# Attention and gated MLP on one core: the first keys loaded in two parts, identity transposes while the first data are on their way

## The chip, the core and the metric

The kernel runs on one core of a Trainium2 chip. TensorE (PE) multiplies and transposes, VectorE (DVE), ScalarE (ACT) and GpSimd (POOL) do the elementwise work, SyncE (SP) issues nearly all DMA transfers. The metric is the device time of one execution in microseconds; less is better.

## What is computed

Two steps, all in float32: attention with queries that are averaged in pairs, and an MLP with a gate on its result.

```python
q_pool = q.reshape(4, 8, 576, 2, 64).mean(axis=3)          # q, k, v: 4 batches, 8 heads, 1152 x 64
scores = 1 / np.sqrt(64) * (q_pool @ k.transpose(0, 1, 3, 2))
attn = np.exp(scores - scores.max(-1, keepdims=True))
attn = attn / (attn.sum(-1, keepdims=True) + 1e-9)
x = (attn @ v)                                             # put together to 2304 tokens x 512
h = x @ w_in                                               # 512 x 2048
out = (h * np.clip(h + 3, 0, 6) / 6) @ w_out               # 2048 x 512
```

## The kernel before

Two heads make a pair; there are 16 pairs g, four in each batch. Of a pair, `load_k`, `load_q` and `load_v` fetch keys `kr` (128 partitions x 9 rows x 2 heads x 64), queries `qr` and values `vr`. `pool_q` adds neighbouring queries to `qp`, `turn_q` transposes them on PE (six transposes into PSUM), `keep_q` copies the result to `qh`; `turn_k` and `keep_k` do the same with the keys (nine transposes, `kT`). `scores` multiplies one of nine key tiles with 288 queries of both heads into a PSUM tile `pv`; `keep` copies it to `s` on ACT, and `most` keeps the running maximum `m` on DVE. When nine tiles are through, `fold`, `best` and `spread` (PE, DVE, PE: `pst`, `mq`) take the maximum over the keys, `lessen` subtracts it (DVE or POOL), `expo` is the exponential on ACT, and `values` multiplies with `vr` into `pav`.

The first five pairs (EARLY = 5) run in this form, three PSUM tiles `pv` wide. In the same stretch the two weight matrices are converted: for 16 blocks f and two halves, `load_raw` fetches `raw`, and `convert` has seven steps: ACT makes the absolute value, POOL clamps it, DVE does three passes over bits in a PSUM tile, then ACT or POOL rounds and POOL subtracts; `save_w` writes `w_d`. For f below 12 these three DVE passes use a `pv` tile.

After the maxima of the fifth pair and the conversions of the first twelve blocks a step `second_step` gives the PSUM of `pv` to other tiles. From there the other eleven pairs run in another form (`pqk`, `pt`), and between their steps the layers of the MLP (`do_layer`, tile `ph`; `do_project`, tile `po`). After the last pair only MLP layers are left.

The order of all this is set by a planner. `arrange` lists every step with a place (from tables of numbers: START, SLOPE, AT, ATL, BIAS and so on), its cost on each engine that may do it, the steps it needs, and the buffers it takes and frees. `Order.run` plays this list through in time: an engine that is free takes, of the steps that are ready and have room, the one with the lowest place. The instructions are then written down in that order, and each engine works its own list in order; a waiting instruction holds up all behind it.

In the first pair nine keys come in one load of two transfers (one for each head, on SP's queue), the queries in one transfer that ACT issues. `turn_k` of the first five pairs is split in six and three tiles, since one PSUM tile holds six. In the listing `load_raw` for f = 0 needs the step `lq` of pair 0 to be placed.

Of the kernel before, what the change touches and what calls it, by code (L numbers as in the profile page):

```python
# [11 lines left out]
F32 = mybir.dt.float32  # L12
# [9 lines left out]
SWEEPS = ((0, 0, 8), (1, 0, 8), (0, 8, 16), (1, 8, 16), (2, 0, 16), (3, 0, 16), (4, 0, 16), (5, 0, 16))  # L22
START = (477.66, 415.01, 302.76, 744.89, 190.23, 357.45, 457.74, 517.76)
SLOPE = (-25.05, 17.09, -28.37, -75.02, 10.14, 11.96, 19.53, -7.47)
LAG = 21.74
MLP = (-241.92, 155.01, -282.2, -587.9)
CONV = 836.78
CSTEP = (77.41, -722.1)
NEAR = 5
EARLY, FCV = 5, 12  # L30
BIAS = (-271.81, -258.65, 75.37, -576.39, 171.43, 165.5)
CUT = 8
PER = (13.78, 18.27)
AT = (104.48, -27.88, 1.45, 269.18, -487.99, 83.52, -374.87, 520.32, -503.94, -3.26, -120.1, 156.6, -61.98, 354.49)
ATL = (36.18, -16.61, -201.47, 878.58, 286.63, 413.95, -133.32, -449.41, 489.14, 426.77, 869.98, 263.26, 385.08, 499.61)
TAIL = 768
QUEUED = True
STICK = 0.2926
# [9 lines left out]
class Order:  # L48
# [10 lines left out]
    def run(self):  # L59
# [11 lines left out]
        back, out, t, wires = [], [], 0.0, 0.0  # L71
# [10 lines left out]
        while len(out) < len(steps):  # L82
# [4 lines left out]
            for e in engines:  # L87
# [17 lines left out]
                if e == "PE":  # L105
                    more, kind = SHIFT.get((kind, cost[e][3]), 0), cost[e][3]
                    busy, end = busy + more, end + more
                    while work and work[0][1] < t - SPELL:
                        work.pop(0)
                    idle = SPELL - sum(max(0.0, min(y, t) - max(x, t - SPELL)) for x, y in work)  # L110
                    if not slow:
                        slow = t > 16000 and idle > IDLE
                        since = t
                    elif t - since >= SPELL and idle < 340:
                        slow = False
                    if slow:
                        busy, end = 2 * busy, end + busy
                    work.append((t, t + busy))
# [37 lines left out]
def arrange(od, do, B=4, NPAIR=4, KT=9, KC=3, NH=2, NFC=16, NT=2304, P=128, HQ=288, SQ=576):  # L156
# [8 lines left out]
    for g in range(NG):  # L165
# [3 lines left out]
        early = g == 0  # L169
        add(("lk", g), lead + at[11], {"SP": (940, 6500, 2600)}, do("load_k", g=g), (), ("kr",))  # L170
        add(("lq", g), lead + at[12], {"SP": (470, 6900, 2000)}, do("load_q", g=g), (), ("qr",))
        z = lead + at[0]
# [5 lines left out]
        for c in C3 if late else range(2):  # L178
            n = 3 if late or c else 6
            add(("tk", g, c), z + 2 + c, {"PE": (100 * n, 100 * n + 250, 0, "t") if late else (160 * n, 160 * n + 300, 0, "t")}, do("turn_k", g=g, c=c),  # L180
                [("tk", g, c - 1)] if c else [("lk", g)] + [("second",)] * (g == NEAR), ("v" if g < NEAR else "s",),
                ("kr",) if c == (2 if late else 1) else ())
# [17 lines left out]
        for h in range(NH):  # L200
            for j in range(2):
# [3 lines left out]
                if late or j == 0:  # L205
                    before = (g, h, 0) if j else (g, h - 1, late) if h else (g - 1, NH - 1, g - 1 >= EARLY) if g else None
                    for t in range(KT):
# [3 lines left out]
                            ([("mm", u, t - 1)] if t else [("mm", before, KT - 1)] if before else [])  # L211
                            + ([("ql", g, h, j) if late else ("qh", g, 0, 0)] if not t else []) + [("kl", g, t // KC) if late else ("kh", g, t // 6)]
                            + ([("second",)] if late and not t else []),
# [138 lines left out]
def pooled_attention_then_gated_mlp(ctx, tc, q, k, v, w_in, w_out, out):  # L352
# [5 lines left out]
    KC = 3  # L358
# [122 lines left out]
    with ExitStack() as a:  # L481
# [32 lines left out]

        def load_k(eng, g):
            kr_t[g] = ld.tile([P, KT, 2, D], F32, tag="kr", name="kr", bufs=1)
# [36 lines left out]
        def space(g, *shape):  # L553
# [3 lines left out]
            return ps_m["s"].tile([P] + list(shape), F32, tag="s", name="pt")  # L557

        def turn_k(eng, g, c):
            if g < EARLY:  # L560
                ps = room_v()[:, :, 0:KC * P].rearrange("p b (t k) -> p b t k", k=P)
                to = [ps[:, t // KC, t % KC, :] for t in range(6)]
                ts = range(6 * c, min(6 * c + 6, KT))
            else:
# [7 lines left out]
        def keep_k(eng, g, c):  # L572
# [5 lines left out]
            if g < EARLY:  # L578
                n = 1 if c else 2
                to = kT[g][:, 6 * c:6 * c + KC * n].rearrange("p (b t) k -> p b (t k)", t=KC)  # L580
                copy(eng, to, ps[:, 0:n].rearrange("p b t k -> p b (t k)"))
                return
# [425 lines left out]
```

## Time and profile before

| | |
|---|---|
| time, median of 3 runs | 872.42 us (872.12 to 872.78) |
| the profiled execution: time, span | 872.05 us, 870.0 us |
| mean granted clock of PE | 0.987 |
| PE busy in the span | 837.8 us (96%) |
| DVE busy | 666.7 us (77%) |
| ACT busy | 574.4 us (66%) |
| POOL busy | 507.5 us (58%) |

A busy time is the time in which at least one instruction of the engine is under way. Matmuls are pipelined and their ends are modelled, so a busy PE can still be one that could do more. The span runs from the first to the last instruction; the 2.05 us between it and the time of the execution lie around it. Shares are means over stages that have different limits, so the profile has to be read stretch by stretch.

### The profile page before, as it was taken

Reading aid. Unit: us, or ns where it says so; the run is one execution under the profiler, and the core shown is the slowest. Engines: PE = TensorE matmul, PEld = TensorE weight load, DVE = VectorE, ACT = ScalarE, POOL = GpSimd, SP = SyncE. Lnnn points to the kernel's source line nnn. Section 1 sums busy time; section 2 is a strip of 40 time slices with the busy share of each in tenths; the row PEclk is TensorE's granted clock in tenths of the full one; section 3 lists DMA queues with packets and bytes.
Section 4 is the critical chain, followed back from the end, with each engine's and each line's share of the span. In section 5 each row is a group of like instructions: output and inputs, shape, how many; then the busy total and the mean of one; then the engine's idle time right before and its main releaser. Section 6 shows DMA issues by size and latency. Waiting matters only on the chain.

```text
span 870.0 us, 16219 instructions
## 1 busy us (share of the span) xinstructions
PE 837.8 (96%) x5668; PEld 648.7 (75%) x5668; DVE 666.7 (77%) x1318; ACT 574.4 (66%) x1222; POOL 507.5 (58%) x457
## 2 busy tenths in 40 slices
PE   4899999999999999999999999999999999999997
PEld 3445555556888886888888878888888877888886
DVE  3898999987999989888889898888988973222222
ACT  3789897885777776767767777777767754222222
POOL 1756777775876785678568867787655766000000
PEclk9699999989999999999999999999999999999999
DMA  9878675569976896799777968898766748343423
GB/s 232 290 238 252 220 221 185 197 222 290 311 243 223 252 324 191 242 282 332 220 247 252 287 206 251 283 293 273 218 204 223 240 147 295 121 131 118 139 99 95
DMA packets 108976, 197.66 MB, mean 227 GB/s; under 512 B 46176, under 2 KB 63584, under 8 KB 108896
## 3 DMA queue, kind: packets, MB, share of 16 engines
q1 hardware_dynamic: 108208, 195.26, 70.3%
q10 hardware_dynamic: 688, 1.38, 0.5%
q8 instruction: 45, 0.74, 0.3%
q14 instruction: 35, 0.29, 0.1%
HBM read 168.82 MB, written 27.79 MB: 226 GB/s over the span
## 4 chain that ended last, share of the span: by engine, by line
PE 68%; DVE 11%; POOL 7%; issue 7%; ACT 5%; DMA 2%; SPq 0%; DVEq 0%; POOLq 0%; ACTq 0%
PE ph L408 20%; PE po L441 14%; PE pav L726 12%; PE pqk L630 10%; PE pt L441 5%; DVE m L648 4%; POOL d L719 3%; PE pv L626 3%; DVE s L701 2%; ACT s L535 2%; ACT s L709 1%; POOL gl L426 1%; PE pt L604 1%; PE pt L570 1%; DMA raw<-in_moe_w_out_dram 1%
## 5 line engine op out<-in xcount | busy, mean ns | idle before, releaser
L709 ACT ACTIVATE s<-s 128x864 f32<-128x864 f32 x192 | 177.2, 931 | 19.7 <-DVE s L701 17.8
L408 PE MATMUL ph<-mxmxh,w 128*128 128x256 f32 x896 | 180.8, 285 | 1.0 <-DVE r L417 0.7
L701 DVE TENSOR_TENSOR s<-s,pst 128x864 f32<-128x864 f32 x168 | 173.8, 1043 | 1.8 <-ACT mb L535 1.2
L535 ACT COPY s<-pqk 128x288 f32<-128x288 f32 x396 | 143.6, 403 | 39.5 <-PE pqk L630 37.5
L648 DVE TENSOR_TENSOR m<-pqk,m 128x288 f32<-128x288 f32 x308 | 138.1, 448 | 28.3 <-ACT s L535 17.9
L726 PE MATMUL pav<-s,vr 128*64 128x288 f32 x1152 | 155.3, 415 | 0.7 <-DVE x L797 0.6
L408 PEld LDWEIGHTS ph<-mxmxh,w 128*128 128x128 f32 x896 | 146.5, 190 | 4.4 <-DVE r L417 2.0
L413 ACT ACTIVATE r<-ph,three 128x256 f32<-128x256 f32 (+1 forms) x128 | 64.1, 501 | 114.4 <-PE ph L408 112.3
L441 PE MATMUL po<-w,gh 128*128 128x512 f32 x448 | 139.2, 392 | 0.0
L408 PE MATMUL ph<-mxmxl,w 128*128 128x256 f32 x448 | 126.4, 282 | 0.0
L726 PEld LDWEIGHTS pav<-s,vr 128*64 128x64 f32 x1152 | 77.8, 138 | 59.2 <-issue 12.1
L417 DVE SCALAR_TENSOR_TENSOR r<-r,ph 128x256 f32<-128x256 f32 (+1 forms) x128 | 56.8, 444 | 84.9 <-ACT r L413 84.4
L719 POOL TENSOR_TENSOR d<-s 128x864 f32<-128x864 f32 x44 | 91.0, 2069 | 52.5 <-ACT s L709 52.5
L630 PE MATMUL pqk<-qh,kT 128*128 128x288 f32 x396 | 119.6, 318 | 2.1 <-DVE m L648 1.9
L426 POOL TENSOR_TENSOR gl<-r,gh 128x256 fp32r<-128x256 f32 x96 | 70.9, 739 | 68.8 <-ACT gh L421 68.5
L630 PE MATMUL pqk<-ql,kT 128*128 128x288 f32 x396 | 110.8, 294 | 0.0
L441 PEld LDWEIGHTS po<-w,gh 128*128 128x128 f32 x448 | 84.3, 188 | 14.4
L441 PE MATMUL po<-w,gl 128*128 128x512 f32 x224 | 90.6, 404 | 1.5 <-DMA w<-w_d 1.0
L630 PEld LDWEIGHTS pqk<-qh,kT 128*128 128x128 f32 x396 | 74.6, 188 | 23.1 <-issue 7.9
L719 POOL TENSOR_TENSOR d<-d,s 128x864 f32<-128x864 f32 x44 | 90.1, 2048 | 1.6 <-ACT s L709 0.6
L408 PEld LDWEIGHTS ph<-mxmxl,w 128*128 128x128 f32 x448 | 85.2, 190 | 1.0
L421 ACT CAST gh<-r 128x256 fp32r<-128x256 f32 (+1 forms) x128 | 55.7, 435 | 32.7 <-DVE r L417 27.0
(107 smaller groups left out, 1415.9 us busy)
## 6 DMA issues: line engine op xcount, KB each, us to landing
w<-w_d SPq DMA_DIRECT2D x224, 512.0 KB, 5.0
w_d<-scratch SPq DMA_DIRECT2D x32, 512.0 KB, 4.6
kr<-in_k_dram SPq DMA_DIRECT2D x32, 288.0 KB, 6.2
vr<-in_v_dram SPq DMA_DIRECT2D x16, 576.0 KB, 4.3
qr<-in_q_dram SPq DMA_DIRECT2D x15, 576.0 KB, 7.3
raw<-in_moe_w_in_dram SPq DMA_DIRECT2D x16, 512.0 KB, 4.1
raw<-in_moe_w_out_dram SPq DMA_DIRECT2D x16, 512.0 KB, 5.9
mxmxh<-xh_d SPq DMA_DIRECT2D x5, 512.0 KB, 6.6
```

The source lines that it names most:

```text
L408: nc.tensor.matmul(ps, w[:, wi, cs], x[:, c, :], start=(m == 0), stop=(m == 3 * NCC - 1))
L413: nc.scalar.activation(out=r6, in_=ps, func=AF.Relu, bias=three)
L417: nc.vector.scalar_tensor_tensor(out=out, in0=r6, scalar=6.0, in1=ps, op0=ALU.min, op1=ALU.mult)
L426: on.tensor_tensor(out=gl, in0=r6, in1=gh.bitcast(F32), op=ALU.subtract)
L441: nc.tensor.matmul(o, g[:, ts], w[:, wi, :], start=(first and n == 0), stop=(last and n == 2))
L535: nc.scalar.copy(out=out, in_=in_)
L630: nc.tensor.matmul(ps[:, 0:HQ], kT[g][:, j, t, :], w[:, j, :], start=(m == 0), stop=(m == 1))
L648: nc.vector.tensor_tensor(out=m, in0=ps, in1=s0 if t == 1 else m, op=ALU.max)
L701: by[eng].tensor_tensor(out=s, in0=s, in1=m.unsqueeze(1).to_broadcast([P, KC, HQ]), op=ALU.subtract)
L709: nc.scalar.activation(out=s, in_=s, func=AF.Exp, scale=SCALE)
L719: by[eng].tensor_tensor(out=out, in0=x, in1=y, op=ALU.add)
L726: nc.tensor.matmul(av_t[g, h][j * D:(j + 1) * D, :], vr_t[g][:, j, t, :], s_t[g, h][:, j, t, :], start=(t == 0), stop=(t == KT - 1),)
```

## The change

The first pair gets its own loads. `load_k` takes a range of key tiles; for pair 0 there are two loads, tiles 0 to 2 (step `l0`) and tiles 3 to 8 (`lk`), each of two transfers. `first_k` splits the transposes and copies of pair 0 in three and six tiles instead of six and three. The place of `turn_q` in pair 0 is put ahead. A new step `warm` writes 36 transposes of the identity into a `pv` tile that nothing reads. The raw load of block 0 no longer needs `lq` of pair 0. All tables of the planner have new numbers, and with them the order of the whole program; the stretch at the start in which the planner does not count with a slow PE is 8 us instead of 16.

```diff
-START = (477.66, 415.01, 302.76, 744.89, 190.23, 357.45, 457.74, 517.76)
+START = (319.41, 415.74, 585.3, 658.57, 427.45, 490.94, 433.17, 512.16)
...
-SPELL, IDLE = 3413, 1600
+SPELL, IDLE, COLD = 3413, 1600, 8000
...
-                        slow = t > 16000 and idle > IDLE
+                        slow = t > COLD and idle > IDLE
...
+        if early:
+            add(("wu",), -1000, {"PE": (6400, 6400, 0, "t")}, do("warm"), (), ("v",), ("v",))
+            add(("lq", g), -1000, {"SP": (100, 5700, 1900)}, do("load_q", g=g), (), ("qr",))
+            add(("l0",), -999, {"SP": (800, 4500, 700)}, do("load_k", g=g, t0=0, t1=KC), (), ("kr",))
+            add(("lk", g), -998, {"SP": (800, 7000, 1300)}, do("load_k", g=g, t0=KC, t1=KT))
+        else:
+            add(("lk", g), lead + at[11], {"SP": (940, 6500, 2600)}, do("load_k", g=g), (), ("kr",))
+            add(("lq", g), lead + at[12], {"SP": (470, 6900, 2000)}, do("load_q", g=g), (), ("qr",))
...
-            n = 3 if late or c else 6
+            n = 3 if late or c != early else 6
...
-            z = place(g) + 2 * UNIT * h - at[1]
+            z = -900 if early else place(g) + 2 * UNIT * h - at[1]
...
-            add(("lr", f, h), z - 8, {"SP": (470, 6300, 1700)}, do("load_raw", f=f, half=h), ([("mm", (0, 0, 0), 2)] if f else [("lq", 0)]) + ([("cv", f - 2, 1 - h, 4)] if f > 1 else []), (f"raw{h}",))
+            add(("lr", f, h), z - 8, {"SP": (470, 6300, 1700)}, do("load_raw", f=f, half=h), ([("mm", (0, 0, 0), 2)] if f else []) + ([("cv", f - 2, 1 - h, 4)] if f > 1 else []), (f"raw{h}",))
...
-                nc.sync.dma_start(out=kr_t[g][:, :, j, :], in_=k[b, h].rearrange("(p t) d -> p t d", p=P))
+                nc.sync.dma_start(out=kr_t[g][:, t0:t1, j, :], in_=k[b, h].rearrange("(p t) d -> p t d", p=P)[:, t0:t1])
+
+        def warm(eng):
+            v = room_v()
+            for x in range(36):
+                nc.tensor.transpose(v[:, 0, 0:P], ident, ident)
...
+        def first_k(g, c):
+            cuts = (0, KC if g == 0 else 2 * KC, KT)
+            return cuts[c], cuts[c + 1]
```

What this does to the instructions is shown at three places. A row is one or more instructions of one engine in the order in which it works them, with line, operation, output and inputs, shape and count. The lines of the changed kernel are up to 16 higher.

PE at the start of the program, before: transposes of the keys and queries of pair 0, then its scores, and the first `fold`.

```order
L570 MATMUL pv<-ident,kr 128x128 x9
L599 MATMUL pv<-ident,qp 128x96 x6
L626 MATMUL pv<-qh,kT 128x288 x24
L674 MATMUL pst<-ident,m 96x128 x3
L626 MATMUL pv<-qh,kT 128x288 x4
```

And now:

```order
L531 MATMUL pv<-ident 128x128 x36
L586 MATMUL pv<-ident,kr 128x128 x3
L615 MATMUL pv<-ident,qp 128x96 x6
L586 MATMUL pv<-ident,kr 128x128 x6
L642 MATMUL pv<-qh,kT 128x288 x22
```

The 36 transposes stand first, the queries' transposes stand between the two parts of the keys.

ACT at the start, before (L535 is the copy helper, L856 the first step of a conversion):

```order
L535 COPY kT<-pv 128x768
L535 COPY kT<-pv 128x384
L535 COPY s<-pv 128x2x288 x4
L856 ACTIVATE scratch<-raw 128x512
L535 COPY s<-pv 128x2x288
L856 ACTIVATE scratch<-raw 128x512
```

And now:

```order
L547 COPY kT<-pv 128x384
L547 COPY qh<-pv 128x576
L872 ACTIVATE scratch<-raw 128x512 x2
L547 COPY s<-pv 128x2x288 x3
L547 CAST scratch<-scratch 128x512
```

The copy of the queries came over from DVE, the larger copy of keys went to DVE, and the first step of both halves of block 0 now stands ahead of the first copy of scores instead of behind the fourth.

DVE from the start of its work on pair 0, before (L648 is the maximum, L864, L869 and L873 the three passes of a conversion):

```order
L545 TENSOR_TENSOR qp<-qr 96x6x64 x2
L537 COPY qh<-pv 128x576
L648 TENSOR_TENSOR m<-pv,s 128x576
L648 TENSOR_TENSOR m<-pv,m 128x576 x3
L864 TENSOR_SCALAR pv<-scratch 128x512
L648 TENSOR_TENSOR m<-pv,m 128x576
```

And now:

```order
L557 TENSOR_TENSOR qp<-qr 96x6x64 x2
L549 COPY kT<-pv 128x768
L880 TENSOR_SCALAR pv<-scratch 128x512
L885 SCALAR_TENSOR_TENSOR pv<-raw,pv 128x512
L664 TENSOR_TENSOR m<-pv,s 128x576
L889 SCALAR_TENSOR_TENSOR scratch<-raw,pv 128x512
```

Two passes of a conversion moved ahead of the first maximum.

## Rows read from the trace of the kernel before

**Rows 1.** Windows: us, busy PE, PEld, DVE, ACT, POOL, PE clock, DMA share, GB/s.
```profile
0.00:19.19 19.19, 9.61 (x43) 6.99 (x43) 5.93 (x20) 7.00 (x11) 1.53 (x8) 1.00 1.03 260
19.19:175.00 155.81, 146.09 (x1140) 79.53 (x1140) 144.19 (x225) 132.51 (x230) 110.14 (x104) 0.96 0.70 224
...
190.00:720.00 530.00, 523.68 (x3653) 431.38 (x3652) 461.31 (x974) 381.96 (x884) 374.40 (x326) 1.00 0.79 252
```

**Rows 2.** Timelines, first 18 us: start, us, engine, line, out<-in, count [idle before].
```profile
1.01 0.29 POOL masks.py:199 TENSOR_SCALAR_AFFINE_SELECT ident<-ident 128x128 f32<-128x128 f32 x1
...
5.57 1.02 DVE L545 TENSOR_TENSOR qp<-qr 96x384 f32<-96x384 f32 x2 [2.91 <-DMA qr<-in_q_dram]
...
8.26 2.15 PE L570 MATMUL pv<-ident,kr 128*128 128x128 f32 x9 [8.26 <-DMA kr<-in_k_dram]
...
12.32 6.49 PE L626 MATMUL pv<-qh,kT 64*128 64x288 f32 x28 [0.94 <-DVE qh L537]
...
13.69 0.64 ACT L535 COPY s<-pv 128x576 f32<-128x576 f32 x1 [2.69 <-PE pv L626]
...
15.32 0.76 DVE L648 TENSOR_TENSOR m<-pv,s 128x576 f32<-128x576 f32 x1 [3.15 <-ACT s L535]
...
17.10 0.67 ACT L856 ACTIVATE scratch<-raw 128x512 f32<-128x512 f32 x1
...
17.86 0.61 POOL L858 TENSOR_SCALAR scratch<-scratch 128x512 f32<-128x512 f32 x1 [16.55 <-ACT scratch L856]
```

**Rows 3.** Windows over the first loads; the last number is GB/s.
```profile
0.00:8.00 8.00, 0.00 (x0) 0.00 (x0) 2.15 (x15) 1.28 (x1) 0.70 (x6) 1.00 0.89 179
8.00:10.00 2.00, 1.74 (x9) 1.77 (x10) 0.00 (x0) 0.19 (x1) 0.00 (x0) 1.00 1.09 373
```

**Rows 4.** PE: scores at 16 to 18 and 18 to 20, transposes, a window.
```profile
L626 PE MATMUL pv<-qh,kT 64*128 64x288 f32 x12 | 2.9, 636 | 0.0
...
L626 PE MATMUL pv<-qh,kT 64*128 64x288 f32 x6 | 1.1, 444 | 0.0
...
37.12 1.17 PE L599 MATMUL pv<-ident,qp 96*128 96x96 f32 x6
...
38.42 1.15 PE L570 MATMUL pv<-ident,kr 128*128 128x128 f32 x9
...
38.00:39.00 1.00, 1.00 (x11) 1.00 (x10) 0.59 (x1) 0.95 (x3) 0.63 (x1) 0.87 0.99 351
```

**Rows 5.** DVE groups by shape, 0 to 175 us; the page's exponential group.
```profile
L701 DVE TENSOR_TENSOR s<-s,pst 128x864 f32<-128x864 f32 x33 | 34.1, 1044 | 0.9 <-ACT mb L535 0.9
L864 DVE TENSOR_SCALAR pv<-scratch 128x512 uint32<-128x512 uint32 x24 | 16.5, 688 | 3.6 <-POOL scratch L858 2.3 <-ACT s L535 0.3
...
L537 DVE COPY qh<-pv 128x576 f32<-128x576 f32 x3 | 2.2, 740 | 4.8 <-PE pv L599 4.8
L537 DVE COPY x<-pav 128x288 f32<-128x288 f32 x3 | 1.4, 450 | 0.0
...
L537 DVE COPY kT<-pv 128x768 f32<-128x768 f32 x1 | 0.9, 912 | 0.0
L537 DVE COPY kT<-pv 128x384 f32<-128x384 f32 x1 | 0.5, 544 | 0.0
...
L709 ACT ACTIVATE s<-s 128x864 f32<-128x864 f32 x192 | 177.2, 931 | 19.7 <-DVE s L701 17.8
```

**Rows 6.** Around the change of stage: a window, and PE's timeline.
```profile
174.00:179.40 5.40, 3.73 (x35) 2.25 (x27) 5.02 (x11) 3.56 (x7) 3.30 (x4) 0.89 0.35 120
...
179.37 3.15 PE L726 MATMUL pav<-s,vr 128*64 128x288 f32 x12 [0.56 <-DVE x L797]
...
186.36 0.46 PE L696 MATMUL pst<-ident,mq 96*128 96x96 f32 x3
186.75 1.68 PE L726 MATMUL pav<-s,vr 128*64 128x288 f32 x12
```

**Rows 7.** DVE's waits from 19.19 to 175 us: total, times, longest.
```profile
DVE m L648 <- ACT s L535: 3.5, 7, 0.9
```

More of the change, by code (lines that the diff above doesn't have):

```diff
@@ L22 @@
 SWEEPS = ((0, 0, 8), (1, 0, 8), (0, 8, 16), (1, 8, 16), (2, 0, 16), (3, 0, 16), (4, 0, 16), (5, 0, 16))
-START = (477.66, 415.01, 302.76, 744.89, 190.23, 357.45, 457.74, 517.76)
[L24 to L28, printed above, removed]
+START = (319.41, 415.74, 585.3, 658.57, 427.45, 490.94, 433.17, 512.16)
+SLOPE = (-17.97, 17.36, -40.58, -56.66, 7.94, 4.7, 11.88, 16.54)
+LAG = 79.73
+MLP = (-210.77, 190.37, -107.71, -694.25)
+CONV = 933.83
+CSTEP = (104.43, -691.1)
 NEAR = 5
 EARLY, FCV = 5, 12
-BIAS = (-271.81, -258.65, 75.37, -576.39, 171.43, 165.5)
+BIAS = (-223.73, -414.45, -161.58, -399.1, 220.5, 285.78)
 CUT = 8
-PER = (13.78, 18.27)
-AT = (104.48, -27.88, 1.45, 269.18, -487.99, 83.52, -374.87, 520.32, -503.94, -3.26, -120.1, 156.6, -61.98, 354.49)
-ATL = (36.18, -16.61, -201.47, 878.58, 286.63, 413.95, -133.32, -449.41, 489.14, 426.77, 869.98, 263.26, 385.08, 499.61)
+PER = (14.57, 17.84)
+AT = (145.72, -51.21, 16.16, 71.58, -630.56, 61.99, -267.56, 606.83, -489.22, -59.04, -21.19, 134.2, -70.67, 375.86)
+ATL = (29.4, -7.25, -165.71, 932.44, 251.82, 417.4, -51.12, -468.16, 419.33, 340.1, 817.81, 256.61, 487.11, 656.69)
 TAIL = 768
 QUEUED = True
-STICK = 0.2926
+STICK = 0.2485
 CT = 256
@@ L178, in arrange @@
         for c in C3 if late else range(2):
-            n = 3 if late or c else 6
+            n = 3 if late or c != early else 6
             add(("tk", g, c), z + 2 + c, {"PE": (100 * n, 100 * n + 250, 0, "t") if late else (160 * n, 160 * n + 300, 0, "t")}, do("turn_k", g=g, c=c),
-                [("tk", g, c - 1)] if c else [("lk", g)] + [("second",)] * (g == NEAR), ("v" if g < NEAR else "s",),
+                ([("tk", g, c - 1)] if c else []) + [("l0",) if early and not c else ("lk", g)] * (early or not c) + [("second",)] * (g == NEAR and not c), ("v" if g < NEAR else "s",),
                 ("kr",) if c == (2 if late else 1) else ())
@@ L211, in arrange @@
                             ([("mm", u, t - 1)] if t else [("mm", before, KT - 1)] if before else [])
-                            + ([("ql", g, h, j) if late else ("qh", g, 0, 0)] if not t else []) + [("kl", g, t // KC) if late else ("kh", g, t // 6)]
+                            + ([("ql", g, h, j) if late else ("qh", g, 0, 0)] if not t else []) + [("kl", g, t // KC) if late else ("kh", g, t // (KC if early and t < 6 else 6))]
                             + ([("second",)] if late and not t else []),
@@ L513, in pair, with load_k @@
             return b, 2 * p + j
[L515 to L516 removed]
+        def load_k(eng, g, t0=0, t1=KT):
+            if t0 == 0:
+                kr_t[g] = ld.tile([P, KT, 2, D], F32, tag="kr", name="kr", bufs=1)
             for j in range(2):
                 b, h = pair(g, j)
[L519 removed]
+                nc.sync.dma_start(out=kr_t[g][:, t0:t1, j, :], in_=k[b, h].rearrange("(p t) d -> p t d", p=P)[:, t0:t1])
[3 more added lines that the diff above has]
+                nc.tensor.transpose(v[:, 0, 0:P], ident, ident)
         def load_q(eng, g):
@@ L562, in turn_k @@
                 to = [ps[:, t // KC, t % KC, :] for t in range(6)]
-                ts = range(6 * c, min(6 * c + 6, KT))
+                ts = range(*first_k(g, c))
             else:
@@ L578, in keep_k @@
             if g < EARLY:
-                n = 1 if c else 2
-                to = kT[g][:, 6 * c:6 * c + KC * n].rearrange("p (b t) k -> p b (t k)", t=KC)
-                copy(eng, to, ps[:, 0:n].rearrange("p b t k -> p b (t k)"))
+                t0, t1 = first_k(g, c)
+                to = kT[g][:, t0:t1].rearrange("p (b t) k -> p b (t k)", t=KC)
+                copy(eng, to, ps[:, 0:(t1 - t0) // KC].rearrange("p b t k -> p b (t k)"))
                 return
```

2 lines of the change are left out of this document (removed).

## The prediction

> **What bounds the kernel now.** I read the windows first, since the shares of the whole span mix three stages. From 190 to 720 us PE is busy 523.68 of 530 us while DVE and ACT have room [rows 1]: there PE is the bound, and a microsecond gained ahead of it is kept if PE's work stays the same. From 19.19 to 175 us, where the first five pairs and the conversions run, DVE is busy 144.19 of 155.81 us (93%), ACT 132.51, and PE issues only 1140 of its 5668 instructions, with modelled ends that make it look full [rows 1]. So DVE is the nearest to a bound there, and PE waits for maxima and copies. In the first 19.19 us DVE is busy for 5.93 us alone [rows 1]: 13.26 us of the engine that bounds the next 156 us go by unused. The timelines say why: the keys land at 8.26, scores start at 12.32, the first maximum stands at 15.32 because ACT's copy of scores comes at 13.69 and later [rows 2]. The change is about this stretch.
>
> PE's clock needs care. The window of the first 19 us reads 1.00 [rows 1], but nine key transposes take 2.15 us at 8.26 [rows 2] and 1.15 us at 38.42 [rows 4], and scores fall from 636 to 444 ns between 16 to 18 and 18 to 20 us [rows 4]. Until about 18 us PE is at the lower of its two levels, 1.2 GHz, whatever the row prints.
>
> **The start, step by step.** The 36 identity transposes need the identity, ready at 1.30 [rows 2]. At four times nine they cost 8.6 us on the lower level [rows 2] and 4.6 us on the upper one [rows 4]. PE waits for data until 8.26 anyway [rows 2], so up to 7 us are free. No row says where in the run the clock would rise; I take the middle, 6.6 us, and PE is free at 8.0. The first keys: three tiles, a third of the bytes, so they are there before that; they cost 3/9 of 1.15, 0.4 us (PE at 8.4). The six query transposes, priced like key transposes, take 0.8 (9.2); their input, the sums on DVE, is done at 6.59 [rows 2]. The other six key tiles take 0.8 more (10.0); their bytes come with the whole of the keys, at 8.1 to 8.3 as before, with PE not there yet.
>
> ACT then copies the queries (the same size as a copy of scores, 0.64 [rows 2]): 9.3 to 9.9. Now the two first conversion steps stand ahead of every copy of scores, and they wait for the raw weights. Queries and keys have 0.59 MB each, a raw half 0.52 MB; these four make 2.2 MB. By 8.0 us 1.43 MB had moved and by 10.0 another 0.75 [rows 3], and the values, which stood between the two raw halves, now come behind them. So the second half lands at about 10.2, and ACT, which reaches it at 10.6 (0.67 for the first [rows 2]), hardly waits; it is through at 11.2. Two copies follow, to 12.5. DVE copies the keys (0.91 [rows 5]) from 10.2, POOL clamps 0.61 [rows 2] behind 10.6, and two conversion passes of 0.69 [rows 5] fill DVE to about 12.6, when the first maximum starts. Until then DVE has done 2.15 [rows 3] + 0.91 + 1.38 = 4.4 us and idled 8.2. Before, 13.26 us were idle until it was loaded at 19.19. At the 7% idle of the later stretch, the time between 12.6 and 19.2 costs 0.5. **The start gives 13.26 - 8.2 - 0.5 = 4.6 us.** Bounds: with every transpose on the upper level PE is free at 5.9 and ACT's wait for the second raw half sets the pace (10.2 + 0.67 + 2 x 0.64 = 12.2), 5.0 us. With all on the lower level PE is free at 9.9, and 15 transposes at 0.24 take it to 13.5; queries are copied at 13 at the latest, two conversion steps and two copies put the first maximum at about 15.6, and the start gives 13.26 - 11.2 - 0.3 = 1.8 us.
>
> **What else moved up to the last maximum of the fifth pair.** I counted DVE's list up to it in both orders. New: one conversion (three passes of about 0.69, 2.06), one copy of 768 keys (0.91), three of 384 (1.63). Gone: one subtraction (1.04), two query copies (1.48), three copies of values (1.35) [rows 5]. Together +0.7 us. PE's list up to the last scores of that pair lacks one block of twelve value matmuls (1.68) and one `spread` (0.46) [rows 6]: 2.1 us that come later, where PE is the bound.
>
> **At the change of stage** PE is idle 5.40 - 3.73 = 1.67 us between 174 and 179.4, and then works at a lowered clock: twelve value matmuls take 3.15 us where they take 1.68 [rows 6]. In the new order a whole MLP layer stands right behind the last `fold`, where PE waited. I book the idle 1.67 as gone. That the clock then also stays up would be worth up to 1.5 for this block; I book half, 0.7, because nothing in the trace shows which.
>
> Behind that, both orders have the same instructions (the only new ones are the 36 transposes, and two DMA issues), and matmuls of attention and of the MLP are mixed in nearly the same proportion at each point of PE's list; the shortest distance from the end of a layer to its projection is longer than before. I put the rest of the replanning at nothing, with 1.5 us to either side, an estimate: a quarter of the 6.3 us that PE idles between 190 and 720 [rows 1].
>
> Sum: 4.6 - 0.7 - 2.1 + 1.7 + 0.7 = 4.2 us. Against the profiled execution, 872.05 - 4.2 = 867.85; the median of the runs lies 0.37 above that execution: **868.2 us**. By bounds: 1.8 - 0.7 - 2.1 + 0 + 0 - 1.5 = a loss of 2.5; 5.0 - 0.7 - 2.1 + 1.7 + 1.5 + 1.5 = a gain of 6.9.
>
> **The rivals.** *The identity transposes do not bring the clock up.* They would then end at 9.9, later than the keys, and the start gives 1.8 instead of 4.6: 871.0, no change that can be seen. For it: the 2.15 us of transposes from 8.26 [rows 2] and the queries' behind them did not lift the clock, since scores still took 636 ns between 16 and 18 us [rows 4]. Against it: the clock came back between 38 and 39 us, while PE was doing transposes, as it had since 37.12 [rows 4], though scores stood ahead of them. The Trainium skill, in "TensorE: Matmul & The Clock Gate", Part 4: PE-mode transpose, says that work in transpose mode does not count as activity for the full clock; by that rule this rival is the outcome, and the trace agrees with it at 8.26 and speaks against it at 38 us.
>
> *The gain is lost on DVE's neighbours.* DVE was 93% busy, not 100: if POOL and ACT, which has 85% [rows 1], take over as bound of the first stage, the 4.6 us turn into more waits of DVE: 872, the same. For it speaks that 1.38 us of the gain are conversion passes done early, which only helps where DVE is last; against it that DVE has the least room of the three.
>
> *Slower: exponentials ahead of copies of scores.* ACT works its list in order, and a maximum needs its copy. DVE waited for such a copy 7 times between 19.19 and 175, 3.5 us [rows 7]. Each exponential that stands ahead of a copy that DVE wants costs up to 0.93 [rows 5]. 90 copies are placed anew; if five of them stand wrongly, the 4.2 us are gone; from seven on (868.2 + 6.5 = 874.7) it would be measured as slower, and with nine it is 876.6. Against it: what stands between the copies of the first two pairs is much as it was.
>
> **How the numbers follow.** Less than 0.2% (1.7 us) cannot be told from no change here; so faster is below 870.7 and slower above 874.2. Forecast 0.62, nine tenths of it faster (0.56) and the rest, near its lower bound, the same (0.06). Clock rival 0.16, a third of it faster (0.05), the rest the same (0.11). Lost on the neighbours 0.12, the same. Slower order 0.10. Together faster 0.61, same 0.29, slower 0.10. The range begins at 865.0, just below the upper bound of the gain (872.4 - 6.9 = 865.5), and ends at 872.8, behind the cases at 871.0 and 872; the slower order and the worst of the lower bound are left out.
>
> **What would show it.** Right: scores start near 10 us rather than 12.32, the first maximum near 12.6, DVE busy about 10 us in the first 19.19; the first scores at less than 500 ns; the first MLP layer earlier by 5 us or more. If the transposes run 240 ns apart to the end and the first scores at 700 ns, the clock rival holds. If the first stage gains 4 us and the time doesn't, the replanned order after 190 us lost it: PE's idle time from 190 to 720, 6.3 us now, would have grown. If DVE's waits for copies grow beyond 3.5 us, it is the last rival. Wrong altogether would be a second raw half that lands near 13: ACT would stand still with all copies behind it.

## The result: 9.9 us faster, more than twice what was forecast

| | before | after |
|---|---|---|
| median of the runs | 872.6 us (872.12 to 873.37) | 862.98 us (861.49 to 864.59) |
| ratio to before, 95% interval | | 0.9886 (0.987 to 0.9903) |
| the profiled execution: time, span | 872.05, 870.0 us | 863.9, 862.1 us |

The forecast was 868.2 us, with a range from 865.0 to 872.8: the change is faster than the lower end. Below, differences in us are (ratio - 1) x 872.6 with the interval of the ratio, so this one is -9.9 (-11.3 to -8.5); the medians differ by 9.6, the figure in some of the expectations.

The start came nearly as it was put down. These are rows of the timeline of after around the first maximum (start, duration, instruction, idle time before it and its releaser), answering to [rows 2]:

```profile
1.36 6.80 PE L531 MATMUL pv<-ident 128*128 128x128 f32 x36 [1.36 <-POOL ident masks.py:199]
8.00 0.49 PE L586 MATMUL pv<-ident,kr 128*128 128x128 f32 x3
8.33 0.66 PE L615 MATMUL pv<-ident,qp 96*128 96x96 f32 x6
8.83 0.82 PE L586 MATMUL pv<-ident,kr 128*128 128x128 f32 x6
9.72 0.76 PE L642 MATMUL pv<-qh,kT 64*128 64x288 f32 x4
11.38 0.66 ACT L872 ACTIVATE scratch<-raw 128x512 f32<-128x512 f32 x1 [1.02 <-DMA raw<-in_moe_w_out_dram]
13.15 0.76 DVE L664 TENSOR_TENSOR m<-pv,s 128x576 f32<-128x576 f32 x1 [0.63 <-ACT s L547]
13.96 2.29 PE L642 MATMUL pv<-qh,kT 64*128 64x288 f32 x8 [0.58 <-DVE m L664]
```

The 36 transposes take 6.80 us (6.6 assumed), scores start at 9.72 instead of 12.32, four of them in 0.76 us, and the first maximum at 13.15 (12.6 assumed) instead of 15.32. The second raw half, forecast for about 10.2, kept ACT waiting until 11.38. The clock did not stay up: the eight scores from 13.96, behind waits of PE, take 2.29 us, the pace of the lower level (in one of the runs below, 16 take 2.24 us on the upper one), and the first window below has a granted clock of 0.86. The windows of after (busy time and instructions of PE, PE's weight loads, DVE, ACT and POOL, then PE's granted clock, DMA share, GB/s) answer to [rows 1, 6]:

```profile
0.00:19.19 19.19, 15.21 (x79) 11.48 (x81) 10.15 (x27) 8.34 (x13) 5.12 (x11) 0.86 1.02 252
19.19:175.00 155.81, 141.37 (x1105) 76.70 (x1101) 141.12 (x218) 130.67 (x230) 107.58 (x102) 0.98 0.72 235
174.00:179.40 5.40, 4.90 (x58) 2.90 (x55) 3.43 (x6) 3.83 (x8) 3.86 (x2) 1.00 0.34 112
175.00:220.00 45.00, 44.43 (x378) 32.61 (x379) 40.40 (x83) 36.45 (x81) 30.66 (x31) 1.00 0.81 262
190.00:720.00 530.00, 527.59 (x3702) 433.24 (x3699) 462.76 (x977) 384.22 (x884) 380.69 (x332) 1.00 0.80 255
```

and these stretches of before were not among its rows:

```profile
175.00:190.00 15.00, 13.48 (x82) 8.53 (x83) 13.52 (x24) 11.84 (x25) 10.46 (x11) 0.77 0.58 206
175.00:220.00 45.00, 41.70 (x312) 28.55 (x312) 35.76 (x74) 30.72 (x71) 30.16 (x31) 0.92 0.81 261
190.00:220.00 30.00, 28.22 (x233) 20.02 (x231) 22.24 (x51) 18.89 (x47) 19.70 (x21) 1.00 0.93 288
```

Two readings. First, DVE's work done by 175 us is 10.15 + 141.12 = 151.3 us, in before 5.93 + 144.19 = 150.1 [rows 1]: of 4.2 us that DVE won by 19.19 us, 3.1 are idle again by 175. One trace of each says this only roughly: nine traces with the old start and old first stage have 5.9 to 7.4 us done by 19.19 and 149.4 to 151.0 by 175; the four with the new ones have 10.1 to 10.5 and 151.3 to 152.2. DVE's waits for copies of scores, from 19.19 to 175 us, grew from 3.5 us in 7 waits [rows 7] to this (total, times, longest):

```profile
DVE m L664 <- ACT s L547: 5.5, 12, 1.1
```

Second, the first MLP layer starts at 178.77 us instead of 189.26 (5 us or more were named), and from 175 to 220 us after gets 40.40 us of DVE's work and 44.43 of PE's done where before gets 35.76 and 41.70. So the question was whether the start brought the gain at all, and what the new order does behind 175 us.

### The profile page after: what moved, and what is told of

It reads as the page before. It is cut to its first block, busy times and chain, and to the rows that moved or that the text cites. A ratio compares the mean times of both kernels' runs of the same rounds, so it can differ in the third digit from the quotient of the medians.

```text
span 862.1 us, 16285 instructions
## 1 busy us (share of the span) xinstructions
PE 835.0 (97%) x5704; PEld 648.8 (75%) x5704; DVE 667.3 (77%) x1319; ACT 574.1 (67%) x1222; POOL 507.8 (59%) x456
## 4 chain that ended last, share of the span: by engine, by line
PE 77%; DVE 8%; DMA 5%; ACT 4%; issue 3%; POOL 2%; SPq 1%; DVEq 0%; ACTq 0%; POOLq 0%
PE ph L414 22%; PE po L447 16%; PE pav L742 14%; PE pqk L646 12%; PE pt L447 5%; DVE m L664 3%; PE pv L642 3%; DMA w_d<-scratch 2%; DMA w<-w_d 2%; DVE s L717 1%; PE pt L620 1%; ACT s L547 1%; ACT s L725 1%; PE pt L586 1%; PE psr L772 1%
## 5 line engine op out<-in xcount | busy, mean ns | idle before, releaser
L646 PEld LDWEIGHTS pqk<-ql,kT 128*128 128x128 f32 x396 | 74.8, 189 | 2.6
```

Of the source, the lines that this page charges most:

```text
L646: nc.tensor.matmul(ps[:, 0:HQ], kT[g][:, j, t, :], w[:, j, :], start=(m == 0), stop=(m == 1))
```

## Experiments on the start and the first stage

Where a kernel's order was written out, the loop takes a list of steps in place of the planner's; the diffs below then show the list. "Second" is `second_step`, where the PSUM changes hands (about 175 us). The two orders have not issued quite the same steps there: the old one has ten ahead of it that the new one has behind it (reciprocals of the fourth pair, maxima and exponentials of the fifth), and the new one has six ahead of it that the old one has behind (steps of conversions, a save, loads of raw weights). So a kernel that changes order at second also has these steps in places that neither plan had.

```diff
-        for fn, eng in [(lambda eng: None, None)] + od.run():
+        for fn, eng in [(lambda eng: None, None)] + [(od.steps[x // 8][2], ENGINES[x % 8]) for x in ORDER]:
```

**Less of the new start, in the changed kernel.**

```diff
-            for x in range(36):
+            for x in range(1):
```

> The changed kernel with one transpose of the identity in place of 36; nothing else, the order is the same on every engine. It asks what the clock at the start is worth at the end. The prediction's theory (time won at the start goes through to the end): the start then gives 1.8 instead of 4.6 us, so 863.0 + 2.8 = 865.8 us; a run at 863.5 or less speaks against it. The rival (what the start wins is lost again inside the first stage, as the marks of the two traces say: PE is 2.5 us ahead at first and 3 us behind before the end of the stage): 862.5 to 864.0 us, although the first maximum comes 1.5 us or more later.

Measured: 0.9887 (0.9871 to 0.9902), the same as the changed kernel.

```diff
-            for x in range(36):
+            for x in range(1):
...
+            if t1 == KC:
+                return
             for j in range(2):
                 b, h = pair(g, j)
+                t0 = 0
```

> The changed kernel with one transpose of the identity and the first keys in one load again (two transfers of all nine tiles, as before); the order of the steps is the new one. It undoes the new start and leaves the new order. The prediction's theory: 863.0 + 4.6 = 867.6 us. The rival (the gain of 9.6 us comes from the order at and behind the change of stage): 863 to 865 us.

Measured: 0.9881 (0.9866 to 0.9897). Without transposes and without the split load the changed kernel keeps all of its gain: in this kernel these two parts of the new start give nothing. The order of the first steps, with the conversions ahead of the copies of scores, stays new in this run, and DVE has still done 9.52 us of work by 19.19 (10.15 in the changed kernel, 5.9 to 7.4 with the old start) and 151.5 by 175 (151.3). So most of DVE's early lead comes from that order, and what the transposes and the split add is idle again by 175.

**The new start in the old order.** Only the first steps of the list change:

```diff
-lq0, lk0 (whole), pq0, lr(0,0), tk(0,0), lv0, pq1, lr(0,1), tk(0,1), kh(0,0) ACT, lq1, tq0, lk1, kh(0,1) ACT, qh0 DVE
+wu, lq0, l0, lk0 (rest), lr(0,0), lr(0,1), lv0, pq0, pq1, tk(0,0), tq0, lq1, kh(0,0) ACT, tk(0,1), lk1, qh0 DVE, kh(0,1) ACT
```

> The kernel before with the new start alone (36 transposes, keys in two parts, queries' transposes between them, both raw halves ahead of the values); from the first scores on, every step in the old order. The prediction's term for the start is 4.6 us (1.8 to 5.0): 867 to 868 us with all of it kept. By the mixed kernels (863.96 with the old start, 860.54 with the new one) it should be 3.4 us: 868.5 us. If the old change of stage swallows what comes earlier, 871 us or more.

Measured: 0.9957 (0.9941 to 0.9974), -3.8 us (-5.1 to -2.3). So the start as a whole, with the order of its steps, does give about what was forecast for it. The same start and the old first stage with the new order from second on:

```diff
+ORDER = new start, then the old order to second, then the new order
```

> The new start (36 transposes, keys in two parts, queries between them, both raw halves ahead of the values), then the old order of the first stage from the first scores to second_step, then the new order. The first stage in the old order left DVE practically no idle time between 19 and 178 us, the new one 3 to 5 us. If the start is worth anything where DVE has no idle time left to lose, this beats both: the first maximum about 2 us earlier than in the kernel with the old start and the old first stage (863.96 us), and 861 to 862.5 us at the end. If it ends at 863.5 to 864.5 us, time won at the start is lost at the change of stage too. The prediction's theory (4.6 us of the start kept): 859.5 us.

Measured: 860.54 us, 0.9865 (0.9835 to 0.9896), -11.8 us. This is the mixed kernel of the texts below. Its windows:

```profile
0.00:19.19 19.19, 13.85 (x87) 10.50 (x87) 10.25 (x27) 9.55 (x15) 4.35 (x11) 1.00 1.00 255
19.19:175.00 155.81, 145.61 (x1159) 80.58 (x1160) 143.81 (x226) 131.99 (x229) 109.66 (x104) 0.98 0.70 229
```

DVE has done 154.1 us by 175, 3.9 more than before and 2.8 more than the changed kernel. The two other kernels with this start and the old first stage have 153.9. The old first stage hands on what the start wins; the new one idles most of it away.

**Are the transposes needed for it?** `range(36)` to `range(1)` in that mixed kernel:

> The mixed kernel (new start, old order of the first stage, new order behind second_step: 860.54 us) with one transpose of the identity in place of 36. What the transposes are worth where the first stage keeps what the start gives: by the prediction's two cases of the clock 4.6 - 1.8 = 2.8 us, so 863.3 us; if the clock at the start does not matter (in the new order of the first stage the same edit changed nothing, 861.9 against 863.0 us), 860 to 861 us.

Measured: 860.3 us, 0.9858 (0.9835 to 0.9881): no loss that can be seen, with 2 to 3 us of room in either interval. The start of the two, one transpose first, then 36:

```profile
6.79 0.87 PE L586 MATMUL pv<-ident,kr 128*128 128x128 f32 x3 [4.95 <-DMA kr<-in_k_dram]
7.49 1.22 PE L615 MATMUL pv<-ident,qp 96*128 96x96 f32 x6
8.51 1.48 PE L586 MATMUL pv<-ident,kr 128*128 128x128 f32 x6
9.92 4.58 PE L642 MATMUL pv<-qh,kT 64*128 64x288 f32 x20
```

```profile
1.36 6.19 PE L531 MATMUL pv<-ident 128*128 128x128 f32 x36 [1.36 <-POOL ident masks.py:199]
7.39 0.49 PE L586 MATMUL pv<-ident,kr 128*128 128x128 f32 x3
9.32 2.24 PE L642 MATMUL pv<-qh,kT 64*128 64x288 f32 x16
```

The first part of the keys is there at 6.79, and the 36 transposes hold it up until 7.39 (8.00 in the changed kernel). The scores start only 0.6 us earlier for them, but run faster: from 10 to 11 us one takes 410 ns on the average, and behind a single transpose 684 ns from 11 to 12 us. The first maximum stands at 11.3 instead of 12.9, and DVE has done 1.6 us more by 19.19 (10.25 against 8.65) and 1.2 us more by 175 (154.1 against 152.9). By these traces, one of each kernel, the transposes may be worth about a microsecond here; the times do not show it.

**Is DVE the bound of the first stage?** In the kernel before one pass is done twice:

```diff
-                nc.vector.tensor_scalar(
+                for x in range(2 if half == 0 and 2 <= f < 8 else 1): nc.vector.tensor_scalar(
```

> The kernel before with one pass of DVE (step 2 of a conversion, 0.69 us) done twice in six conversions of the first stage (blocks 2 to 7, first halves): 6 x 0.6 to 0.69 = 3.6 to 4.1 us more work for DVE there, nothing for the other engines, results unchanged. If DVE is the bound of the first stage and the old order has no time to spare, as the prediction reads the windows: 3.6 to 4.1 us slower, about 876 us. If DVE's 7% idle takes it up, or PE: less than 1 us.

Measured: 1.0051 (1.0038 to 1.0064), +4.5 us (3.3 to 5.6). What was added arrives at the end.

## Experiments on where the gain lies

```diff
+ORDER = the new start and order up to second, then the old order
```

> The new start and the new order up to the step that gives the PSUM tiles to other uses (second_step, about 175 us), then the old order for all that is left. All computation is done. The prediction's theory: the 4.6 us of the start are kept and the 2.4 us at the change of stage are not, 868 us or a little more. The rival: the first stage gains nothing, so 871 to 874 us, with the idle time of PE between 190 and 400 us as in the kernel before.

Measured: 1.0028 (1.0012 to 1.0044): slower than before by 2.4 us, on the rival's side and not the prediction's. With the new order behind it the same first part is 2.2 us better than the old one (-9.9 against -7.7 in the next run), so the parts do not add up here. From 175 to 220 us this kernel gets 40.56 us of PE's work and 32.28 of DVE's done, less than before. It changes order at second, so how much of its loss is the new first stage and how much the cut stays open.

```diff
+ORDER = the old start and order up to second, then the new order
```

> The old start and the old order up to second_step, then the new order for all that is left. All computation is done. The prediction's theory: only what it booked at the change of stage, 0.3 to 2.4 us, so 870 to 872 us. The rival: nearly all of the 9.6 us, 862 to 865 us.

Measured: 0.9912 (0.989 to 0.9934), -7.7 us. So most of the gain stands behind second, and with the old first stage it adds up with the start's (-3.8 - 7.7 = -11.5, the mixed kernel has -11.8). The next one exchanges one stretch. At its end both orders have issued the same steps; at its beginning, second, they differ by the sixteen named above, which the expectation overlooks:

```diff
+ORDER = the old order up to second, the new one up to the ninth scores of ('mm', (5, 1, 0)), then the old one
```

> The kernel before with the order of one stretch taken from the changed kernel: from second_step (about 175 us) to the ninth score block of the second half of the sixth pair (220 to 225 us). Both kernels have issued the same steps at either end of it (but for one conversion pass), so nothing else is touched. By the traces PE is 5.1 us ahead at that end once DVE's idle time up to there is counted (14.8 us before, 9.6 after, with 210.6 us of DVE work done in both), and 2.7 us of the gain lie behind it. If DVE's idle time in this stretch is the loss: 5 us less than before, 867 us where before is at 872, and DVE idle some 10 us to its end. If the gain there belongs to the new first stage: 870 us or more.

Measured: 865.98 us, 0.9937 (0.9915 to 0.9958), -5.5 us (-7.4 to -3.7). The profiled execution is the slowest of the six (870.47 us), so its trace shows the gain in part only. From 175 to 220 us DVE gets 38.77 us done and PE 42.15:

```profile
175.00:220.00 45.00, 42.15 (x329) 31.26 (x330) 38.77 (x79) 33.21 (x77) 29.45 (x31) 0.96 0.85 282
```

The remaining 2.2 us of the 7.7 would lie behind 220 us; as a difference of two runs that is uncertain by some 2.7 us to either side. A cut further back says less:

```diff
+ORDER = the new order up to ('mm', (7, 0, 0), 6), about 287 us, then the old one
```

> The new start and the new order up to about 287 us (the seventh score block of the eighth pair), then the old order for all that is left. It splits the gain behind second_step in two. By the marks of the two traces PE is 4.7 us ahead when 250 us of its work are done and 7.8 us at the end: so 865 to 867 us if those marks tell it rightly. If all of the gain comes from the change of stage, 862.5 to 864 us; if it comes from the order of the long stretch behind it, 869 us or more.

Measured: 0.9955 (0.9937 to 0.9973), 6.0 us slower than the changed kernel. Here the two orders do not meet at the cut, and the profiled execution (865.38 us, the lowest of the runs) is not a typical one, so how much of the 6 us is the cut itself stays open.

**Is PE the bound from 190 us on?**

```diff
-            for x, t in zip(to, ts):
+            for x, t in list(zip(to, ts)) * (3 if g in (8, 9) else 1):
```

> The kernel before with the nine transposes of the keys of pairs 8 and 9 (328 to 386 us) done three times over: 36 more transposes at about 0.11 us, 4.0 us more work for PE in the stretch that the prediction calls PE-bound, results unchanged. If PE is the bound there: 4.0 us slower, about 876 us. If PE's waits behind (for maxima and for weights, 2.5 us between 390 and 410 us) take part of it up: 1.5 to 3 us.

Measured: 1.0028 (1.0016 to 1.004), +2.4 us (1.4 to 3.5) for 4.0 added. Not quite: there is room in that stretch.

## Experiments on what the stretch from 175 to 220 us lost

**Work for PE, moved into it.** In the old order:

```diff
 ('tq', 5, 0, 1) PE
+('hd', (0, 0)) PE
 ('av', 4, 0, 0) PE
...
 ('mm', (5, 0, 0), 2) PE
-('hd', (0, 0)) PE
```

> The kernel before with one thing moved: the first MLP layer (its ten matmuls on PE, and its relu, gate, upper and lower part on ACT, DVE and POOL) stands right behind the transposes of the sixth pair's queries, where PE was idle and then worked at the lower clock level (178.4 to 185.2 us), instead of 28 matmuls and transposes later. Theory A (the change of stage costs what it costs because PE has no work there and then runs at the lower level): the clock stays up from 178 on, and of the 1.7 us idle and some 3.2 us of slow work 2 to 5 us come back, 868 to 870 us. Theory B (the gain there needs the whole new order, since the waits only move): 871.5 to 873 us. The prediction's own terms for this place were 1.7 + 0.7 = 2.4 us: 870.2 us.

Measured: 1.0009 (0.999 to 1.0028), nothing. Behind the layer two new waits stand (PE's timeline):

```profile
187.07 0.46 PE L696 MATMUL pst<-ident,mq 96*128 96x96 f32 x3 [0.43 <-DVE mq L684]
190.79 0.37 PE L630 MATMUL pqk<-qh,kT 128*128 128x288 f32 x1 [0.71 <-DVE kT L589]
```

With that layer and two steps more:

```diff
 ('tk', 5, 1) PE
+('hd', (0, 1)) PE
 ('av', 4, 0, 1) PE
 ('s3', (4, 1, 1)) PE
+('pj', (0, 0)) PE
```

> The kernel before with the first two MLP layers and the first projection (some 3.8 us of PE's work that asks DVE for two gates, 0.8 us, only) moved into the stretch from 178 to 188 us, where DVE has more work queued than PE (15.7 us of DVE's work for 10 us of PE's in the old order, 9.2 in the new one), and with their relus and gates on ACT, DVE and POOL. Theory (PE and DVE have to have work in the same proportion all the time; one layer was too little, since the next waits for DVE came at once): 2 to 4 us less than before. If the waits come back behind, as with one layer: no change.

Measured: 1.0007 (0.9995 to 1.002), nothing. The window from 175 to 220 us is no fuller than before:

```profile
175.00:220.00 45.00, 39.94 (x306) 26.41 (x301) 35.39 (x71) 30.73 (x70) 29.01 (x30) 0.96 0.77 249
```

Taking the same work out of the new order costs:

```diff
 ('tq', 5, 0, 1) PE
-('hd', (0, 0)) PE
 ('s3', (4, 1, 0)) PE
...
 ('mm', (5, 0, 0), 2) PE
+('hd', (0, 0)) PE
...
 ('mm', (5, 0, 0), 5) PE
+('hd', (0, 1)) PE
...
 ('o4', 4, 0) PE
+('pj', (0, 0)) PE
```

> The changed kernel with its first two MLP layers and the first projection moved back, behind the third and the sixth block of scores of the sixth pair, and their loads with them; otherwise the new order. Theory A (work for PE at the change of stage is what the new order gains): PE waits and its clock falls near 178 us again, +3 to +6 us, 866 to 869 us. Theory B (something else in the new order makes the gain): 862.5 to 864.5 us.

Measured: 0.9934 (0.9911 to 0.9957), 4.2 us more than the changed kernel. The clock falls as in the old order:

```profile
175.00:190.00 15.00, 13.29 (x99) 9.53 (x91) 10.13 (x21) 11.54 (x25) 10.01 (x8) 0.77 0.45 118
```

So the early layers, with the loads that moved with them, are needed, and they are not enough.

**The clock alone.** Nine identity transposes in the waits (`fill` is called behind three steps), and three transposes of queries done three times:

```diff
+        def fill():
+            for x in range(3):
+                nc.tensor.transpose(st_t["fill"][:, 0, 0:P], ident, ident)
...
-            for t in range(TQ):
+            for t in list(range(TQ)) * (3 if (g, h, j) == (5, 0, 1) else 1):
```

> The kernel before with nine identity transposes in three waits of PE between 175 and 177.6 us (three in each, into a free tile) and the three transposes of the sixth pair's queries done three times over, so that PE has something to do while it waits; order and results unchanged. If PE's lower clock level from 178.4 to 185.2 us comes from these waits, it disappears, and 24 value matmuls, 9 transposes and a block of scores run at twice the pace: up to 3.2 us less at that place. If that carries to the end: 869 us or a little more, against 872. If other engines hold PE there anyway (as with the early layer): no change.

Measured: 1.0006 (0.9994 to 1.0018), nothing, though the clock does stay up. The windows, then the waits behind (PE's timeline):

```profile
174.00:179.40 5.40, 4.91 (x46) 3.57 (x42) 5.02 (x11) 3.56 (x7) 3.29 (x4) 1.00 0.37 128
178.00:190.00 12.00, 9.86 (x75) 6.26 (x73) 10.90 (x18) 9.87 (x21) 9.63 (x10) 1.00 0.62 220
```

```profile
182.83 0.55 PE L570 MATMUL pt<-ident,kr 128*128 128x128 f32 x3 [1.14 <-DVE scratch L884]
188.61 0.37 PE L630 MATMUL pqk<-qh,kT 128*128 128x288 f32 x1 [0.71 <-DVE kT L589]
```

From 178 to 190 us DVE is busy 10.90 of 12 us, as in before, and PE, now at the upper level (1.00), waits for it. The slow clock had been filling time in which PE would have stood still.

**A wait of PE, taken away.** In the old order PE waits 1.42 us at 214.03 for `rw`, which stands on ACT behind a conversion step whose raw weights land at 212.9:

```diff
-('cv', 15, 0, 0) ACT
 ('rw', 4, 1) ACT
 ('re', (0, 2)) ACT
+('cv', 15, 0, 0) ACT
```

> The kernel before with one instruction of ACT moved: the first step of a conversion that waits 1.86 us for its raw weights at about 212 us, and with it the widening of a reciprocal (rw) for which PE stands still 1.42 us at 214.03 us, now stands behind that widening and the next relu. It asks whether a wait of PE in the stretch behind the change of stage carries to the end. If so, 1.4 us less than before, 870.5 us where before is at 871.9; if the wait only moves, no change.

Measured: 1.0003 (0.999 to 1.0016), nothing. The wait on PE at 214 is gone and stands 2 us later, since DVE has the next pass of the same conversion in its list:

```profile
216.34 0.40 PE L630 MATMUL pqk<-qh,kT 128*128 128x288 f32 x1 [1.42 <-DVE m L648]
```

```profile
DVE pcv L864 <- POOL scratch L858: 2.5, 1, 2.5
```

Then with DVE's passes moved too, and a load of weights issued ahead of a store that waits in SP's queue:

```diff
-('cv', 15, 0, 2) DVE
 ('mx', (5, 0, 1), 8) DVE
+('cv', 15, 0, 2) DVE
...
+('lw', (2, 0), 1) SP
 ('sp', 8, 0) SP
-('lw', (2, 0), 1) SP
```

> The kernel before with the causes of two waits of PE taken away. At 214 us: the first three conversion steps of the block whose raw weights land at 212.9 us go behind the work that is ready, on ACT (as in the run that moved ACT's step alone) and now on DVE too, where the same raw weights held up the next maxima. At 398 us: a load of weights is issued ahead of a store of results on SP that waits 3.04 us in the queue. Both waits together are 1.42 + 1.0 = 2.4 us. If waits of PE behind the change of stage carry to the end once the common cause is moved: 2.4 us less than before (with the second wait up to 3.7 less, since it grew to 2.3 us where PE came earlier). If they only change their place again: no change.

Measured: 1.0005 (0.9992 to 1.0017), nothing. The wait for the weights fell to 0.21 us, but maxima keep PE waiting 0.94 and 1.12 us at 215.5 and 217.3. PE's wait for that load had grown in other runs, so part of a gain upstream can be waited away there. Before, then the new start, the moved `rw` and the exchanged stretch, each in the old order behind:

```profile
398.09 0.47 PE L441 MATMUL po<-w,gl 128*128 128x512 f32 x1 [0.99 <-DMA w<-w_d]
```

```profile
394.75 0.77 PE L447 MATMUL po<-w,gl 128*128 128x512 f32 x1 [2.19 <-DMA w<-w_d]
```

```profile
398.96 0.47 PE L441 MATMUL po<-w,gl 128*128 128x512 f32 x1 [2.27 <-DMA w<-w_d]
```

```profile
395.70 0.47 PE L441 MATMUL po<-w,gl 128*128 128x512 f32 x1 [2.35 <-DMA w<-w_d]
```

**The same kind of move where it helps.** In the mixed kernel ACT waits 1.81 us at a conversion step, and PE 1.3 us for it:

```diff
-('cv', 12, 1, 0) ACT
 ('qh', 5, 0, 0) ACT
 ('qh', 5, 0, 1) ACT
 ('re', (0, 0)) ACT
+('cv', 12, 1, 0) ACT
```

> The mixed kernel with one instruction of ACT moved: the first step of a conversion, which waits 1.81 us for its buffer at 173.5 us with the copies of the sixth pair's queries behind it, now stands behind these copies and the first relu. PE stood still for 1.29 us there because of it. If PE's waits at the change of stage carry to the end one to one: 860.5 - 1.3 = 859.2 us. If they only move, as in the kernel before with the early layer, 860.5 us.

Measured: 859.07 us, 0.985 (0.9832 to 0.9869), -13.1 us: the best of all, and better than the changed kernel by 3 us. The wait `pt <- DVE ql` is gone from PE's list, and only 0.7 us for `gl` came in. That this move is worth its 1.3 us is likely, not shown: the intervals of the two mixed kernels overlap.

**What is shown, and what is not.** DVE's waits from 175 to 222 us, before and then after:

```profile
DVE m L648 <- ACT s L535: 4.0, 3, 1.9
DVE pcv L864 <- POOL scratch L858: 3.3, 2, 2.4
DVE ql L618 <- ACT qh L616: 0.5, 1, 0.5
```

```profile
DVE mq L700 <- PE pst L690: 1.9, 1, 1.9
DVE r L423 <- ACT r L419: 0.9, 1, 0.9
DVE mq L696 <- PE pst L685: 0.7, 1, 0.7
```

In the old order the bound changes sides. Up to 190 us DVE is full (13.52 of 15 us from 175) and PE waits or runs slowly; from 190 to 220 PE is busy for 28.22 of 30 us and DVE for 22.24 only, waiting for scores copied late and for conversions whose weights are on their way. Work that both could have done side by side is done one after the other. The new order has PE-heavy layers where DVE is full, and DVE's work where PE is. The exchange of the stretch shows that its order is worth 5.5 us; that this balance is the reason is an account from the windows. No single move brought any of it in the old order, the one that should have balanced it included, so which part of the arrangement is needed beside the early layers stays open. One rival is untested: the exchange also brings the new order of the loads on SP's queue, of raw and of converted weights, and no run exchanged that alone.

## Why the prediction was wrong

- **The start, 4.6 us (1.8 to 5.0): right where the old first stage stands behind it,** 3.8 us in the old order and 4.1 with the new order behind second (uncertain by some 3 us). In the changed kernel 1.2 us of DVE's lead of 4.2 are left at 175, and the transposes and the split load are worth nothing (0.9881 without them, 0.9886 with). The start's division was wrong too: the clock was to make 2.8 of it, and 36 transposes against one make no difference that can be seen in either order, though in the mixed kernel the traces show 1.2 us at 175. They ran into the data, which were there at 6.79, not 8.26.
- **The first stage, -0.7 and -2.1 (together a loss of 2.8): the size came out, in part by luck.** The changed kernel is 1.8 us slower than the mixed one by the ratios and 2.4 by the medians (the intervals overlap), 2.8 us by DVE's work done at 175. Start and first stage together were put at 1.8 us and measured 2.2 (-9.9 against -7.7). The reason is another: DVE's list did grow by the 0.7 that was counted, but its waits for copies, which the slower rival had named, grew by 2.0 us, from 3.5 to 5.5. No run has the new first stage behind the old start, so its price alone is not measured.
- **The change of stage, 1.7 + 0.7, and the rest of the replanning at 0 with 1.5 to either side: this is the step that failed.** Together they were booked with 2.4 us and measured 7.7 (5.8 to 9.6): 5.5 between 175 and 220 us, the rest behind. The step counted PE's idle 1.67 us and half of a slow block in 5.4 us [rows 6] as all that could be won there, and took PE as the bound from 190 us on from one window of 530 us [rows 1]. Its first 30 us, cut apart in the rows above, have DVE idle for 7.8 us and hold 1.8 of PE's 6.3 us. The quarter of 6.3 us was no bound for an order that also changes what DVE waits for. PE's idle time from 190 to 720 fell from 6.3 to 2.4 us, the sign that the prediction had named for a loss, turned round. And the bookings themselves were not what counted: with a layer moved into the waits, or with the clock held up, nothing was won. The remark that attention and MLP are mixed in nearly the same proportion everywhere was wrong at this very place: two layers and a projection stand ahead of the sixth pair's first scores now, and none did. Why the whole order wins what no single move did stays open, as said above.
- **DVE as the bound of the first stage: right,** 4.5 us for 3.6 to 4.1 added. **PE as the bound behind: mostly,** 2.4 for 4.0.
- **The clock rival fell:** the transposes did bring the clock up, and the scores ran at the upper level from 9.72, though not beyond 13.96. Its price (871.0) would have been wrong too: with one transpose the changed kernel loses nothing that can be seen. The sign that was held for it, slow scores behind fifteen transposes in before, was that of one execution (last section).

## What to carry to other kernels

When a whole order is planned anew, exchange it stretch by stretch with the old one, at points where both have issued the same steps, before explaining any wait: the wait that a trace shows is often only the place where a shortage comes to light, and mending it moves it a few instructions on. Cut the windows finely at a change of stage: two engines that are each full in one half and idle in the other are a loss that no single wait shows. And a gain at the start reaches the end only if the engine that bounds the next stage has no new wait in it: here the old first stage with the new start and the new rest is some 2 us better than what was planned as a whole, and 3 us, clear of the noise, with one instruction of ACT moved as well.

## What the runs showed of the hardware

Transposes kept PE's clock up and brought it up. With fifteen of them put into waits, nine of the identity and six of queries, and no other work added, the granted clock from 174 to 179.4 us is 1.00 where it was 0.89 [rows 6], and from 178 to 190 us 1.00 where this row of before has 0.72:

```profile
178.00:190.00 12.00, 11.44 (x68) 7.01 (x67) 10.89 (x18) 9.70 (x20) 9.49 (x10) 0.72 0.61 214
```

At the start, behind 36 of them, 16 score matmuls take 2.24 us from 9.32; behind one, 20 take 4.58 us from 9.92, most of them at the lower level. The Trainium skill, in "TensorE: Matmul & The Clock Gate", Part 4: PE-mode transpose, says that work in transpose mode does not count as activity for the full clock; both traces differ from it, and the measurement decides.

When the clock rises differs between executions of the same instructions. In before, behind fifteen transposes from 8.26 us, 28 scores take 6.49 us [rows 2], nearly all at the lower level. The kernel with the new order from second on has the same instructions up to there, and in its trace, behind the same fifteen transposes, the first 16 scores ran at the upper one, and the first maximum stood at 14.3 instead of 15.32:

```profile
12.29 2.24 PE L626 MATMUL pv<-qh,kT 64*128 64x288 f32 x16 [0.94 <-DVE qh L537]
```

So a single trace does not tell what a given piece of work at the start does to the clock, and it need not stay up: in the changed kernel it was down again for the scores from 13.96.

A lowered clock cost nothing where another engine had PE waiting anyway: the value matmuls of the change of stage ran at half pace in before, and with the clock up the time was the same to 0.2%.
